# Two rows of h open every layer, and the 64 leftover tokens of batch 0 go behind the first 256 of batch 1

## The chip, the cores and the metric

The kernel runs on one core of a Trainium2 chip. The number that counts is the device time in microseconds (us) of one execution; lower is better. A core has engines that run side by side, each through its own list of instructions: PE (matrix products; PEld is its weight load), DVE (vector), ACT (scalar functions), POOL and SP. SP issues most of the DMA transfers. Results of PE land in PSUM, in banks of 128x512 fp32 values, from where ACT or DVE must carry them away before a bank is used again.

## What is computed

Attention over 4 batches, 8 heads, 576 tokens and 64 values a head, where each token keeps its 32 largest scores, and then two layers of a feed-forward network over all 2304 tokens:

```
scores = scale * np.matmul(q, k.transpose(0, 1, 3, 2))
kth = np.partition(scores, -top_k, axis=-1)[..., -top_k:-top_k + 1]
scores = np.where(scores >= kth, scores, -1000000000.0)
attn = softmax of scores;  x = attn @ v, as (2304, 512)
h = np.maximum(x @ w_in, 0.0);          x = h * h @ w_out          # layer 0
h = x @ w_in;  g = np.maximum(0.01 * h, h);  out = g @ w_out       # layer 1
```

Both layers have 512 features in and out and 2048 between them.

## The kernel before

**Attention.** Two heads make a head pair, so there are four head pairs (hp 0 to 3), and the output of head pair c is the 128-feature chunk c of x. `UNITS` lists (batch, first token, tokens); each unit is worked head pair by head pair, in tiles of 128 rows of scores by 576 keys, 144 tiles in all. Two tiles make a pair, 72 pairs in all, and the program is written in slots, 16 to a pair. In each pair DVE finds the 32 largest of every row with 8 MAX8 and 6 MATCH_REPLACE8 (lines 846 and 848). ACT then makes the exponentials (lines 303 and 307), PE transposes them (lines 321 and 334), ACT and DVE carry the transposes to PT or PTs (lines 326 to 344), and PE multiplies by v (line 405 or 416). Batches 2 and 3 have their scores computed during the first 245 slots, kept in DRAM (`sd`) and loaded again later; the others have theirs computed about two pairs ahead (line 285). Units numbered below `NATIVE` multiply by v in plain fp32 (`av`, line 405), the others in two fp32r parts, a high and a low one (`av_split`, line 416), for which v is split into two parts first (`load_v`, `split_v`).

**Feed-forward layers.** Tokens are cut into six `BLOCKS` of 512, 256, 384, 512, 256 and 384. A phase (j, layer) of block j has 16 steps f. Step f makes one row of h: 12 matmuls of a chunk of x (high part xh, low part xl) with the weights wi (line 592). ACT and POOL make gh and gl from it (lines 602 to 618), and one step later 12 (or fewer) matmuls add these into the accumulators acc (lines 635 and 637). At the end of layer 0 ACT and DVE write the accumulators back into x as xh and xl (lines 648 and 649), and layer 1 reads that. The phases run in the order (0,0), (0,1), (1,0), (1,1), (2,0), (2,1), (3,0), (3,1), (4,0), (5,0), (4,1), (5,1). The row h has one PSUM bank, the accumulators have four. In the phases (0,0) and (0,1) every step also converts its weights from 64-bit values (ACT lines 512, 521 and 532, DVE lines 527 and 528, called bits here, POOL line 533) and stores them in DRAM (`wd`); later phases load them from there.

**What sets the order.** A block's phases are written into the program once the block is full; the loop deals out three matmuls at a time at a rate that is meant to end when the next block is full, and writes what is left when it is. Attention work has a higher priority (`SOON`). From that program a list scheduler makes one fixed order for each engine, and each engine then goes through its order. In the order before, block 1 takes the 64 last tokens of batch 0 and 192 of batch 1, and 64 tokens are left over for block 2 (`spill`, `unspill`).

Of the kernel before, what the change touches and what calls it, by code (L numbers as in the profile page):

```python
# [8 lines left out]
F = mybir.dt.float32  # L9
# [3 lines left out]
OP = mybir.AluOpType  # L13
# [11 lines left out]


UNITS = [
    (0, 0, 256), (0, 256, 256), (0, 512, 64), (1, 0, 256), (1, 256, 320),
    (2, 0, 256), (3, 0, 256), (2, 256, 320), (3, 256, 320),
]  # L30

BLOCKS = [512, 256, 384, 512, 256, 384]

SETS = (0, 1, 0, 1, 0, 2)

# [2 lines left out]
SPILL = 128  # L38


NATIVE = 3

EARLY = (2, 3)
FILL = (2, 245)
# [13 lines left out]
LEAD = 24  # L58

SOON = 100  # L60
CONVP = 30

HI_SET = (0, 1, 2, 3, 4, 5, 6, 7, 8, 9, 10, 11, 12, 13, 14, 15)
# [17 lines left out]
def topk_attention_moe_moe2_kernel(  # L81
# [52 lines left out]
    for u in units:  # L134
        for hp in range(NHP):
            n = u["n"]
            uh = dict(u=u, hp=hp, n=n, b=u["b"], first=(u["t0"] == 0), ti=len(tiles), idx=len(uhs),
                      c0=P * (hp % 2) if n == 64 else 0)
# [12 lines left out]
    NPAIRS = len(tiles) // 2  # L151

    def direct(uh):
        return uh["b"] not in EARLY

    for i, uh in enumerate([uh for uh in uhs if direct(uh)]):
        uh["di"] = i

    def split(uh):
# [37 lines left out]
    def at(slot, fn, *a):  # L197
        events.setdefault(slot, []).append((fn, a))
# [68 lines left out]
    def scores(t, half):  # L267
        uh = t["uh"]
        d = uh["qs"]
        kt = KT[uh["b"], uh["hp"]]  # L270
        if half == 0:
            if direct(uh):
                t["s"] = sbufs[t["i"] % NS]
            else:
                t["s"] = ahead.tile([P, S], F, tag="stage", name="stage", bufs=NST)
        ks = slice(half * HALF, (half + 1) * HALF)
        mm = [(x[:, h, c:c + P], kt[:, h, ks]) for h, c in t["parts"] for x in d]
        if not direct(uh):
            ps = stage_psum.tile([P, 512], F, tag="sp", name="sp", bufs=SPB)
        elif uh["b"] == 0:  # L280
            ps = stage_psum.tile([P, 512], F, tag="sd", name="sd", bufs=SDB)
        else:
            ps = bank()
        for i, (l, r) in enumerate(mm):
            PE.matmul(ps[:, 0:HALF], lhsT=l, rhs=r, start=i == 0, stop=i == len(mm) - 1)
        ACT.activation(t["s"][:, ks], ps[:, 0:HALF], AF.Copy, scale=0.125)  # L286
        if half == 1 and not direct(uh):
            t["sd"] = dram.tile([P, S], F, tag=f"sd{t['i']}", name=f"sd{t['i']}")
            SP.dma_start(t["sd"], t["s"])

# [279 lines left out]
    def moe(j, layer):  # L570
# [6 lines left out]
        for f in range(NF + LAG):  # L577
            conv = iter(())
            if f < NF:
# [2 lines left out]
                conv = w_convert(si + 2)  # L582
                w_load(si + 2)
                wi, wo = wt.pop(si)
                h = late["psum"].tile([P, 512], F, tag="h", name="h", bufs=1)
                cnt = 0
# [4 lines left out]
                for w, c, y in mm:  # L591
                    PE.matmul(h[:, 0:n], lhsT=wi[:, w, c * P:(c + 1) * P], rhs=x[c][y][:, 0:n], start=cnt == 0,  # L592
                              stop=cnt == 3 * NK - 1)
                    cnt += 1
                    if cnt % MQ == 0 and cnt < 3 * NK:
                        next(conv, None)
                        yield
                gh = late["mlp"].tile([P, 512], R, tag="gh", name="gh", bufs=2)
                gl = late["mlp"].tile([P, 512], R, tag="gl", name="gl", bufs=2)
                a = late["mlp"].tile([P, 512], F, tag="ga", name="ga", bufs=2)  # L600
# [60 lines left out]
    used = {}  # L661
    opened = 16 * (max(uh["last"] for uh in uhs if not split(uh)) // 2) + 35

    def score_slot(ti):
        return 16 * (ti // 2) - DLEAD + 5 * (ti % 2)

    def after(z, *keys):
        return max([z] + [used[k] + 1 for k in keys if k in used])

    order = []  # L670
    for uh in uhs:
        b, hp, i = uh["b"], uh["hp"], uh.get("di")
        z = score_slot(uh["ti"])
        if uh["first"] and direct(uh):
            st = {"i": i}
            st["n"] = len(order)
            order.append(b)
            z0 = after(z - 62, ("kraw", st["n"] - KRB), *[("KT", x, hp) for x in range(b)])
            at(z0, load_k, b, hp, st)
            for h in range(2):  # L680
                at(z0 + 12 * h + 11, split_k, b, hp, st, h)
            used["kraw", st["n"]] = z0 + 23
            assert z0 + 24 <= z
        if (b, hp) not in vdone or split(uh) and VTB < NHP:
            assert not uh["u"]["i"] < NATIVE <= units[max(x["i"] for x in units if x["b"] == b)]["i"]
            vdone.add((b, hp))
            zv = z + DLEAD + 4
# [16 lines left out]
        used["q", i] = used["KT", b, hp] = score_slot(uh["last"]) + 2  # L704

    later_uhs = {}
    for uh in uhs:
# [44 lines left out]
    for p in range(NPAIRS):  # L752
# [1 line left out]
        pairs.append(pr)  # L754
        z = 16 * p
        for i, t in enumerate(pr["t"]):
            if direct(t["uh"]):
                at(z - DLEAD + 5 * i, scores, t, 0)
                at(z - DLEAD + 2 + 5 * i, scores, t, 1)
            else:  # L760
                at(z - LEAD + i, load_s, t)
            if i == 0:
                at(z + 14, shifts, pr)
            at(z + 14 + i, drop, pr, i)
# [157 lines left out]
```

## Time and profile before

| | us |
|---|---|
| median of 3 runs | 1200.16 |
| lowest and highest run | 1199.25, 1202.18 |
| the profiled execution | 1201.19 |
| its span, first to last instruction | 1199.4 |
| end of the last MAX8 of the 72 pairs | 958.3 |
| first matmul of phase (3,0), block 3 | 731.77 |

PE is busy 1130.8 us of the span, DVE 945.1, ACT 796.4, POOL 678.9; the granted clock of TensorE averages 0.983. Up to about 965 us attention and the feed-forward phases run together; what follows is feed-forward work alone. A row of the timeline gives the start, the length, engine, line, the operation, what it writes and reads, the shapes, how many were merged, and in brackets how long the engine was idle just before and what ended that.

### The profile page before, as it was taken

Reading aid. Unit: us, or ns where it says so; the run is one execution under the profiler, and the core shown is the slowest. Engines: PE = TensorE matmul, PEld = TensorE weight load, DVE = VectorE, ACT = ScalarE, POOL = GpSimd, SP = SyncE. Lnnn points to the kernel's source line nnn. Section 1 sums busy time; section 2 is a strip of 40 time slices with the busy share of each in tenths; the row PEclk is TensorE's granted clock in tenths of the full one; section 3 lists DMA queues with packets and bytes.
Section 4 is the critical chain, followed back from the end, with each engine's and each line's share of the span. In section 5 each row is a group of like instructions: output and inputs, shape, how many; then the busy total and the mean of one; then the engine's idle time right before and its main releaser. Section 6 shows DMA issues by size and latency. Waiting matters only on the chain.

```text
span 1199.4 us, 20071 instructions
## 1 busy us (share of the span) xinstructions
PE 1130.8 (94%) x6388; PEld 989.3 (82%) x6388; DVE 945.1 (79%) x1944; ACT 796.4 (66%) x1787; POOL 678.9 (57%) x922
## 2 busy tenths in 40 slices
PE   5899958999899999999998999999999999999997
PEld 4777846887677789988998997888788899998896
DVE  7999999879879899999999999999999910110121
ACT  6999979789889977766656676555666653334322
POOL 7967575778788875467665664555455543005200
PEclk9999988999999999999998999999999999999999
DMA  9868565679889888899987888676677589779973
GB/s 309 277 213 266 201 218 214 234 290 338 305 296 326 281 298 288 282 333 369 326 308 251 283 279 265 206 232 221 203 231 232 184 277 369 249 250 345 353 253 124
DMA packets 105914, 323.24 MB, mean 270 GB/s; under 512 B 16977, under 2 KB 25169, under 8 KB 101713
## 3 DMA queue, kind: packets, MB, share of 16 engines
q1 hardware_dynamic: 103168, 317.24, 77.6%
q10 hardware_dynamic: 2640, 4.72, 1.1%
q8 instruction: 52, 0.85, 0.3%
q14 instruction: 54, 0.43, 0.1%
HBM read 254.54 MB, written 67.37 MB: 268 GB/s over the span
## 4 chain that ended last, share of the span: by engine, by line
PE 69%; ACT 10%; DVE 10%; DMA 5%; POOL 3%; issue 2%; ACTq 0%; SPq 0%; POOLq 0%; DVEq 0%
PE h L592 28%; PE acc L637 14%; PE acc L635 14%; DVE m L846 4%; PE att L416 4%; PE att L321 3%; DVE w L848 3%; PE att L405 2%; DMA wraw<-in_w_dram 2%; ACT e L303 1%; DMA kraw<-in_k_dram 1%; ACT e L307 1%; DMA out_dram<-y 1%; ACT s L286 1%; ACT stage L286 1%
## 5 line engine op out<-in xcount | busy, mean ns | idle before, releaser
L592 PE MATMUL h<-xh,wi 128*128 128x512 f32 (+2 forms) x1280 | 351.8, 347 | 8.6 <-ACT ga L602 3.5
L846 DVE MAX8 m<-w 128x8 f32<-128x576 f32 x432 | 313.6, 747 | 1.3
L592 PEld LDWEIGHTS h<-xh,wi 128*128 128x128 f32 x1280 | 227.3, 191 | 37.1 <-ACT ga L602 5.0
L848 DVE MATCH_REPLACE8 w<-m,w 128x576 f32<-128x576 f32 x288 | 213.5, 743 | 0.8
L592 PE MATMUL h<-xl,wi 128*128 128x512 f32 (+2 forms) x640 | 207.1, 342 | 2.7 <-DVE xl L649 2.6
L618 POOL TENSOR_TENSOR gl<-ga,gh 128x512 fp32r<-128x512 f32 (+2 forms) x160 | 163.0, 1019 | 43.3 <-ACT gh L617 38.9
L635 PE MATMUL acc<-gh,wo 128*128 128x512 f32 (+2 forms) x768 | 157.4, 342 | 0.3 <-ACT y L652 0.3
L637 PE MATMUL acc<-wo,gh 128*128 128x512 f32 x576 | 151.9, 398 | 2.5 <-ACT gh L617 2.5
L615 POOL TENSOR_TENSOR ga<-ga,gb 128x512 f32<-128x512 f32 (+2 forms) x80 | 81.5, 1018 | 122.3 <-ACT gb L614 122.3
L635 PEld LDWEIGHTS acc<-gh,wo 128*128 128x128 f32 x768 | 127.1, 189 | 12.4 <-ACT y L652 0.8
L592 PEld LDWEIGHTS h<-xl,wi 128*128 128x128 f32 x640 | 121.4, 191 | 14.9 <-DVE xl L649 4.3
L303 ACT ACTIVATE e<-s,m 128x576 f32<-128x576 f32 x144 | 112.4, 781 | 31.1 <-DVE m L846 24.2
L637 PEld LDWEIGHTS acc<-wo,gh 128*128 128x128 f32 x576 | 103.9, 188 | 22.9 <-ACT gh L617 4.0
L307 ACT ACTIVATE e<-e,nb 128x576 f32<-128x576 f32 x144 | 110.9, 774 | 5.7 <-POOL nb L297 5.5
L604 POOL TENSOR_TENSOR ga<-ga 128x512 f32<-128x512 f32 (+2 forms) x80 | 66.3, 828 | 82.3 <-ACT gh L603 79.6
L846 DVE MAX8 m<-s 128x8 f32<-128x576 f32 x144 | 103.7, 747 | 7.9 <-ACT s L286 5.9
L848 DVE MATCH_REPLACE8 w<-m,s 128x576 f32<-128x576 f32 x144 | 107.0, 743 | 0.6
L321 PE MATMUL att<-ident,e 128*128 128x128 f32 x576 | 88.1, 279 | 18.1 <-ACT e L307 12.8
L321 PEld LDWEIGHTS att<-ident,e 128*128 128x128 f32 x576 | 69.7, 143 | 31.2 <-ACT e L307 17.4
L602 ACT ACTIVATE ga<-h 128x512 f32<-128x512 f32 (+2 forms) x80 | 39.1, 488 | 80.2 <-PE h L592 77.8
L316 POOL TENSOR_SCALAR e<-e,rc 128x576 f32<-128x576 f32 x108 | 79.7, 751 | 16.6 <-DVE rc L312 15.4
L617 ACT ACTIVATE gh<-ga 128x384 fp32r<-128x384 f32 (+2 forms) x112 | 58.6, 523 | 42.2 <-POOL ga L615 32.2
(94 smaller groups left out, 2133.4 us busy)
## 6 DMA issues: line engine op xcount, KB each, us to landing
wi<-wd SPq DMA_DIRECT2D x160, 512.0 KB, 5.2
wo<-wd SPq DMA_DIRECT2D x160, 512.0 KB, 5.4
wraw<-in_w_dram SPq DMA_DIRECT2D x32, 1024.0 KB, 6.6
sd<-stage SPq DMA_DIRECT2D x72, 288.0 KB, 3.3
s<-sd SPq DMA_DIRECT2D x72, 288.0 KB, 4.6
wd<-wi SPq DMA_DIRECT2D x32, 512.0 KB, 5.6
wd<-wo SPq DMA_DIRECT2D x32, 512.0 KB, 6.0
kraw<-in_k_dram SPq DMA_DIRECT2D x16, 576.0 KB, 4.5
```

Source lines behind the costliest of these rows:

```text
L303: ACT.activation(t["e"], t["s"], AF.Prelu, bias=pr["m8"][:, i, 31:32], scale=-1.0, alpha=1.0 / FAR)
L307: ACT.activation(e, e, AF.Exp, bias=pr["nb"][:, i:i + 1], scale=-FAR, accum_out=pr["sum"][:, i:i + 1])
L316: POOL.tensor_scalar(e, e, pr["rc"][:, i:i + 1], 1.0, op0=OP.mult, op1=OP.mult)
L321: PE.transpose(ps[:, j * P:(j + 1) * P], t["e"][:, j * P:(j + 1) * P], ident)
L592: PE.matmul(h[:, 0:n], lhsT=wi[:, w, c * P:(c + 1) * P], rhs=x[c][y][:, 0:n], start=cnt == 0, stop=cnt == 3 * NK - 1)
L604: POOL.tensor_tensor(a[:, 0:n], a[:, 0:n], a[:, 0:n], op=OP.mult)
L615: POOL.tensor_tensor(a[:, 0:n], a[:, 0:n], b[:, 0:n], op=OP.subtract)
L618: (DVE if j >= GLD else POOL).tensor_tensor(gl[:, 0:n], a[:, 0:n], gh.bitcast(F)[:, 0:n], op=OP.subtract)
L635: PE.matmul(acc[c][:, 0:n], lhsT=wo[:, w, cs], rhs=g[:, 0:n], start=first, stop=last)
L637: PE.matmul(acc[c], lhsT=g[:, cs], rhs=wo[:, w, :], start=first, stop=last)
L846: cur["dve"] = DVE.max(out=m8[:, x, 8 * r:8 * r + 8], in_=t["s"] if r == 0 else t["w"])
L848: cur["dve"] = DVE.match_replace(out=t["w"], in_to_replace=m8[:, x, 8 * r:8 * r + 8], in_values=t["s"] if r == 0 else t["w"], imm_value=NEG)
```

## The change

- `UNITS`: the unit of the 64 last tokens of batch 0 moves behind the first 256 tokens of batch 1. Block 1 is then exactly these 256 tokens, block 2 is 64 + 320 tokens, and nothing is spilled at block 1.
- `NATIVE` goes from 3 to 2: units 0 and 1 stay plain, and the 64-token unit is now split in two parts as the units after it. Its v is loaded, split and stored a second time.
- `KEPT`: the scores of these 64 tokens are computed while the keys of batch 0 are still there, stored in DRAM and loaded again, as for batches 2 and 3.
- `OPENING`: at step 0 of a phase two rows of h (steps 0 and 1) are computed together, chunk by chunk, the second one in a bank of the accumulators; step 1 then has no matmuls of h left.
- `SEAM`: the evictions from acc to xh and xl at the end of layer 0 get a higher priority.

```diff
 UNITS = [
-    (0, 0, 256), (0, 256, 256), (0, 512, 64), (1, 0, 256), (1, 256, 320),
+    (0, 0, 256), (0, 256, 256), (1, 0, 256), (0, 512, 64), (1, 256, 320),
...
+OPENING = (
+    ((0, 0),), ((1, 0),), ((0, 1),), ((2, 0),), ((1, 1),), ((3, 0),), ((2, 1), (3, 1)),
+)
...
-NATIVE = 3
+NATIVE = 2
+KEPT = 3
...
+SEAM = 400
...
-            if direct(uh):
+            if direct(uh) and not kept(uh):
                 t["s"] = sbufs[t["i"] % NS]
...
-        if half == 1 and not direct(uh):
+        if half == 1 and (kept(uh) or not direct(uh)):
             t["sd"] = dram.tile([P, S], F, tag=f"sd{t['i']}", name=f"sd{t['i']}")
...
                 if f == 0:
-                    mm = [(w, c, 0) for w in range(2) for c in range(NK)] + [(0, c, 1) for c in range(NK)]
+                    two = [late["psum"].tile([P, 512], F, tag="acc" if r else "h", name="h", bufs=4 if r else 1)
+                           for r in range(2)]
+                    ws = [wi, wt[si + 1][0]]
+                    mm = [(r, w, c, y) for part in OPENING for r in range(2) for c, y in part
+                          for w in ((0,) if y else (0, 1))]
+                elif f > 1:
+                    two = [late["psum"].tile([P, 512], F, tag="h", name="h", bufs=1)]
+                    ws = [wi]
+                    mm = [(0, 0, c, y) for c in range(NK) for y in range(2)] + [(0, 1, c, 0) for c in range(NK)]
                 else:
-                    mm = [(0, c, y) for c in range(NK) for y in range(2)] + [(1, c, 0) for c in range(NK)]
+                    mm = []
...
-                ACT.activation(xh[:, 0:n], acc[c][:, 0:n], AF.Copy)
-                DVE.tensor_tensor(xl[:, 0:n], acc[c][:, 0:n], xh.bitcast(F)[:, 0:n], op=OP.subtract)
+                with tc.high_priority(offset=SEAM):
+                    ACT.activation(xh[:, 0:n], acc[c][:, 0:n], AF.Copy)
+                    DVE.tensor_tensor(xl[:, 0:n], acc[c][:, 0:n], xh.bitcast(F)[:, 0:n], op=OP.subtract)
...
+            if kept(t["uh"]):
+                at(t["uh"]["zs"], scores, t, 0)
+                at(t["uh"]["zs"] + 2, scores, t, 1)
+            if kept(t["uh"]) or not direct(t["uh"]):
+                at(z - LEAD + i, load_s, t)
```

The first place is PE where block 0 becomes full. `e` are exponentials, `rc` their sums' reciprocals, `PT,VN` is the product with v for the last head pair, and `h<-xh0` with 128x512 are rows of h in phase (0,0). Before, with the last product and what follows it:

```order
L405 MATMUL att_2499<-PT_115,VN_1069 128x256 x9
L285 MATMUL att_2533<-KT_2187,q00_77 128x288
L285 MATMUL att_2533<-KT_2187,q10_78 128x288
L355 MATMUL att_2484<-ident_66,rc_2295 128x128 x2
L405 MATMUL att_2499<-PT_115,VN_1069 128x256
L285 MATMUL att_2563<-KT_2187,q00_77 128x288
L285 MATMUL att_2563<-KT_2187,q10_78 128x288
L321 MATMUL att_2585<-ident_66,e0_107 128x128 x4
L592 MATMUL h_2543<-xh0_649,wi_2350 128x512 x5
L592 MATMUL h_2543<-xl0_650,wi_2350 128x512 x4
```

Three of the 12 matmuls of the first row stand ahead of the last product, nine behind it. Now the same place of the changed kernel:

```order
L424 MATMUL att_2561<-PT_115,VN_1069 128x256 x8
L374 MATMUL att_2546<-ident_66,rc_2371 128x128 x2
L424 MATMUL att_2561<-PT_115,VN_1069 128x256 x2
L304 MATMUL att_2597<-KT_1962,q01_83 128x288
L304 MATMUL att_2597<-KT_1962,q11_84 128x288
L304 MATMUL att_2642<-KT_1962,q01_83 128x288
L304 MATMUL att_2642<-KT_1962,q11_84 128x288
L618 MATMUL h_2612<-xh0_649,wi_2420 128x512 x2
L618 MATMUL h_2613<-xh0_649,wi_2500 128x512 x2
L618 MATMUL h_2612<-xl0_650,wi_2420 128x512
L618 MATMUL h_2613<-xl0_650,wi_2500 128x512
L618 MATMUL h_2612<-xl0_650,wi_2420 128x512
```

Eight matmuls on the last chunk of x are left for two rows; the 16 on the first three chunks stand ahead of these lines.

The second place is DVE where phase (1,0) ends and its accumulators are written back (`xl1<-acc`). `m8` and `w` belong to the search for the 32 largest, and `s4` and `s5` are the score tiles of a pair that is just being begun. Before:

```order
L848 MATCH_REPLACE w_6428<-m8_6424,s3_104 128x576
L846 MAX m8_6424<-w_6427 128x8
L846 MAX m8_6424<-w_6428 128x8
L312 RECIPROCAL rc_6222<-sum_6221 128x2
L846 MAX m8_6592<-s4_105 128x8
L848 MATCH_REPLACE w_6427<-m8_6424,w_6427 128x576
L649 TENSOR_TENSOR xl1_2826<-acc_5236,xh1_2825 128x256
L649 TENSOR_TENSOR xl1_2826<-acc_5237,xh1_2825 128x256
```

Counted from the start of DVE's order, 278 of its 576 MAX8 stand ahead of the first of these `xl1` lines. After:

```order
L872 MAX m8_6192<-s4_105 128x8
L872 MAX m8_6050<-w_6054 128x8
L346 TENSOR_TENSOR PTs_2609<-att_5938,PTs_2609 128x4x128
L874 MATCH_REPLACE w_6195<-m8_6192,s4_105 128x576
L346 TENSOR_TENSOR PTs_2609<-att_5956,PTs_2609 128x4x128
L874 MATCH_REPLACE w_6054<-m8_6050,w_6054 128x576
L676 TENSOR_TENSOR xl1_3215<-acc_5075,xh1_3214 128x256
L676 TENSOR_TENSOR xl1_3215<-acc_5076,xh1_3214 128x256
```

Here 256 MAX8 stand ahead of the write-back: it has moved up by 22 MAX8, not quite three pairs, in DVE's order.

The third place is PE where block 3 becomes full and phase (3,0) opens; `acc` with `wo` is the end of phase (2,1), `PTs,VT` the product with v, `h<-xh1` with 128x512 the new phase. Before:

```order
L637 MATMUL acc_8265<-wo_9032,gl_9193 128x512
L637 MATMUL acc_8266<-wo_9032,gl_9193 128x512
L637 MATMUL acc_8267<-wo_9032,gl_9193 128x512
L416 MATMUL att_9230<-PTs_3112,VT_8843 128x256
L321 MATMUL att_9290<-ident_66,e0_107 128x128 x4
L321 MATMUL att_9324<-ident_66,e1_108 128x128 x4
L334 MATMUL att_9352<-ident_66,e0_107 64x128
L334 MATMUL att_9352<-ident_66,e1_108 64x128
L592 MATMUL h_9266<-xh1_7292,wi_9102 128x512 x5
```

The last product with v for block 3 stands beside the last matmuls of phase (2,1). After, a few lines behind the end of (2,1), which now comes one whole head pair earlier:

```order
L435 MATMUL att_9158<-PTs_2609,VT_8919 128x256 x9
L340 MATMUL att_9214<-ident_66,e2_109 128x128 x4
L340 MATMUL att_9239<-ident_66,e3_110 128x128 x4
L353 MATMUL att_9265<-ident_66,e2_109 64x128
L353 MATMUL att_9265<-ident_66,e3_110 64x128
L435 MATMUL att_9311<-PTs_2609,VT_8919 128x256 x9
L618 MATMUL h_9353<-xh1_7376,wi_9194 128x512
```

Both products of the last head pair now stand behind the end of (2,1), with only attention work and the first 16 matmuls of the new phase around them.

## Rows read from the trace of the kernel before

**Rows 1.** The page, part 1: busy us (share of the span) xinstructions.

```profile
PE 1130.8 (94%) x6388; PEld 989.3 (82%) x6388; DVE 945.1 (79%) x1944; ACT 796.4 (66%) x1787; POOL 678.9 (57%) x922
```

**Rows 2.** Windows of two stretches: length, busy us by engine, PE clock, DMA share, GB/s.

```profile
core 0: us, PE busy (x) PEld busy (x) DVE busy (x) ACT busy (x) POOL busy (x), PEclk, DMA share, GB/s
...
316.00:419.00 103.00, 97.71 (x457) 78.22 (x457) 90.43 (x171) 95.23 (x183) 86.00 (x85) 0.98 0.88 307
...
502.00:739.00 237.00, 230.18 (x1387) 213.16 (x1385) 234.27 (x495) 151.22 (x344) 146.41 (x214) 0.99 0.87 303
```

**Rows 3.** What DVE waited for, 193 to 419 us: total us, times, longest.

```profile
DVE wc L527 <- ACT att L521: 19.0, 15, 4.2
DVE m L846 <- ACT s L286: 3.6, 5, 1.4
```

**Rows 4.** The same for DVE, 419 to 739 us, all there is.

```profile
DVE m L846 <- ACT s L286: 1.0, 1, 1.0
DVE PTs L327 <- ACT PTs L326: 0.2, 1, 0.2
DVE xf L422 <- ACT tmp L421: 0.2, 1, 0.2
```

**Rows 5.** Timeline of DVE: first write-back of (1,0), block 3 full, write-back of (3,0).

```profile
501.89 0.75 DVE L649 TENSOR_TENSOR xl<-acc,xh 128x256 fp32r<-128x256 f32 x2
...
738.57 0.43 DVE L422 TENSOR_TENSOR xf<-att,tmp 64x256 f32<-64x256 f32 x1
...
849.74 0.68 DVE L649 TENSOR_TENSOR xl<-acc,xh 128x512 fp32r<-128x512 f32 x1
```

**Rows 6.** What PE waited for, 193 to 502 us: first and last of thirteen.

```profile
PE att L334 <- ACT s L286: 3.0, 1, 3.0
...
PE att L285 <- ACT s L286: 0.2, 1, 0.2
```

**Rows 7.** Timeline of PE where phase (0,0) opens.

```profile
194.34 1.43 PE L592 MATMUL h<-xh,wi 128*128 128x512 f32 x5 [0.49 <-ACT xh L437]
195.61 1.07 PE L592 MATMUL h<-xl,wi 128*128 128x512 f32 x4
197.70 0.66 PE L321 MATMUL att<-ident,e 128*128 128x128 f32 x4 [1.02 <-DVE wc L528]
198.84 0.50 PE L592 MATMUL h<-xh,wi 128*128 128x512 f32 x1 [0.49 <-ACT ga L602]
```

**Rows 8.** Timeline of PE between (0,0) and (0,1), and where (1,0) ends.

```profile
316.24 2.87 PE L592 MATMUL h<-xh,wi 128*128 128x512 f32 x8 [0.18 <-ACT xh L648]
...
319.95 1.09 PE L592 MATMUL h<-xl,wi 128*128 128x512 f32 x2 [0.39 <-DVE xl L649]
...
322.69 0.79 PE L592 MATMUL h<-xh,wi 128*128 128x512 f32 x1 [1.28 <-ACT gb L614]
...
498.71 0.64 PE L635 MATMUL acc<-gl,wo 128*128 128x256 f32 x4
```

**Rows 9.** The chain that ended last, pieces: start us, us, what.

```profile
215.78 4.83 PE att L405 x40
...
322.69 4.56 PE h L592 x12
...
330.48 2.75 PE h L592 x12
```

**Rows 10.** Timeline of PE: prices of a score matmul, a transpose and a split product.

```profile
434.82 0.69 PE L285 MATMUL att<-KT,q 128*128 128x288 f32 x4
...
521.19 1.03 PE L321 MATMUL att<-ident,e 128*128 128x128 f32 x8
...
538.42 1.34 PE L416 MATMUL att<-PTs,VT 128*128 128x320 f32 x8
```

**Rows 11.** Timeline of PE where block 3 becomes full and where (2,0) has ended.

```profile
650.40 1.15 PE L592 MATMUL h<-xl,wi 128*128 128x384 f32 x2 [1.95 <-DVE xl L649]
...
739.06 0.64 PE L334 MATMUL att<-ident,e 128*64 128x128 f32 x2 [1.52 <-DVE xf L422]
```

More of the change, by code (lines that the diff above doesn't have):

```diff
@@ L136, in topk_attention_moe_moe2_kernel @@
             n = u["n"]
-            uh = dict(u=u, hp=hp, n=n, b=u["b"], first=(u["t0"] == 0), ti=len(tiles), idx=len(uhs),
+            uh = dict(u=u, hp=hp, n=n, b=u["b"], first=(u["t0"] == 0), i0=u["i"], ti=len(tiles), idx=len(uhs),
                       c0=P * (hp % 2) if n == 64 else 0)
@@ L154, in direct, with kept, score_slot @@
         return uh["b"] not in EARLY
-    for i, uh in enumerate([uh for uh in uhs if direct(uh)]):
+    def kept(uh):
+        return uh["u"]["i"] == KEPT
+    def score_slot(ti):
+        return 16 * (ti // 2) - DLEAD + 5 * (ti % 2)
+    for uh in uhs:
+        uh["zs"] = score_slot(uh["ti"])
+        if kept(uh):
+            ahead_of = [x for x in uhs if x["b"] == uh["b"] and x["hp"] == uh["hp"] and x["i0"] < uh["i0"]][-1]
+            uh["zs"] = score_slot(ahead_of["last"]) + 5
+    in_time = sorted([uh for uh in uhs if direct(uh)], key=lambda uh: uh["zs"])
+    for i, uh in enumerate(in_time):
         uh["di"] = i
@@ L584, in moe @@
                 wi, wo = wt.pop(si)
-                h = late["psum"].tile([P, 512], F, tag="h", name="h", bufs=1)
-                cnt = 0
                 if f == 0:
-                    mm = [(w, c, 0) for w in range(2) for c in range(NK)] + [(0, c, 1) for c in range(NK)]
-                else:
-                    mm = [(0, c, y) for c in range(NK) for y in range(2)] + [(1, c, 0) for c in range(NK)]
[L591 to L595, printed above, removed]
+                    two = [late["psum"].tile([P, 512], F, tag="acc" if r else "h", name="h", bufs=4 if r else 1)
[7 more added lines that the diff above has]
+                    mm = [(0, 0, c, y) for c in range(NK) for y in range(2)] + [(0, 1, c, 0) for c in range(NK)]
+                else:
+                    mm = []
+                for cnt, (r, w, c, y) in enumerate(mm):
+                    mine = [i for i, m in enumerate(mm) if m[0] == r]
+                    PE.matmul(two[r][:, 0:n], lhsT=ws[r][:, w, c * P:(c + 1) * P], rhs=x[c][y][:, 0:n],
+                              start=cnt == mine[0], stop=cnt == mine[-1])
+                    if cnt % MQ == MQ - 1 and cnt < len(mm) - 1:
                         next(conv, None)
                         yield
+                h = two.pop(0)
                 gh = late["mlp"].tile([P, 512], R, tag="gh", name="gh", bufs=2)
@@ L662, in topk_attention_moe_moe2_kernel @@
     opened = 16 * (max(uh["last"] for uh in uhs if not split(uh)) // 2) + 35
-    def score_slot(ti):
-        return 16 * (ti // 2) - DLEAD + 5 * (ti % 2)
     def after(z, *keys):
@@ L670, in topk_attention_moe_moe2_kernel @@
     order = []
-    for uh in uhs:
+    for uh in in_time + [uh for uh in uhs if not direct(uh)]:
         b, hp, i = uh["b"], uh["hp"], uh.get("di")
-        z = score_slot(uh["ti"])
+        z = uh["zs"]
         if uh["first"] and direct(uh):
@@ L684, in topk_attention_moe_moe2_kernel @@
         if (b, hp) not in vdone or split(uh) and VTB < NHP:
-            assert not uh["u"]["i"] < NATIVE <= units[max(x["i"] for x in units if x["b"] == b)]["i"]
             vdone.add((b, hp))
-            zv = z + DLEAD + 4
+            zv = score_slot(uh["ti"]) + DLEAD + 4
             if split(uh):
@@ L703, in topk_attention_moe_moe2_kernel @@
         used["qraw", i] = z1 + 4
-        used["q", i] = used["KT", b, hp] = score_slot(uh["last"]) + 2
+        used["q", i] = used["KT", b, hp] = (z if kept(uh) else score_slot(uh["last"])) + 2
     later_uhs = {}
@@ L756, in topk_attention_moe_moe2_kernel @@
         for i, t in enumerate(pr["t"]):
-            if direct(t["uh"]):
+            if kept(t["uh"]):
[3 more added lines that the diff above has]
+                at(z - LEAD + i, load_s, t)
+            else:
                 at(z - DLEAD + 5 * i, scores, t, 0)
                 at(z - DLEAD + 2 + 5 * i, scores, t, 1)
-            else:
-                at(z - LEAD + i, load_s, t)
             if i == 0:
```

## Prediction

> **What bounds the kernel now.** I read the page's shares first: PE is busy 94% of the span, DVE 79% [rows 1]. An average hides stages, so I went to the windows and, for each, to the list of what DVE and PE waited for. Three stages come out.
>
> Up to 193 us DVE works through the pairs that fill block 0, and PE has nothing to do but attention. From 193 to 419 us the phases (0,0) and (0,1) run beside attention and convert their weights. DVE waits there for ACT, 19.0 us in 15 waits for the bits and 3.6 for scores [rows 3]; ACT is busy 95.2 of the 103 us from 316, POOL 86.0, PE 97.7 [rows 2]. PE sets the pace here, ACT close behind, and DVE has time over. From 419 to 739 us it is the other way round: DVE waits three times, 1.4 us in all [rows 4], and is busy 234.3 of the last 237 us [rows 2]. PE waits there too (1.95 us at the seam from (2,0) to (2,1) [rows 11]), but these waits end nothing: block 3 is full when DVE has done its work, at 738.57 us [rows 5], and PE, idle for 1.52 us, waits for exactly that [rows 11]. The write-back of (3,0) at 849.74 us [rows 5] comes again from a DVE that was busy throughout. Behind it PE alone counts.
>
> So the end is: the time at which DVE stops waiting, plus DVE's work from there to the write-back of (3,0), plus some 345 us of PE. A PE wait between 419 and 739 us costs nothing now, and nothing is won by taking it away.
>
> **The change, part by part.** By the orders, the last instruction that DVE must wait for PE with moves to the end of phase (1,0), to its write-back. I add up when PE gets there, and what DVE still has to do.
>
> Start: DVE's order has two instructions fewer ahead of block 0's last piece, so 0.8 us less; the first row of h on the last chunk goes from 194.3 [rows 7] to 193.5 us.
>
> PE from there to the end of (1,0) takes 304.8 us before: 194.3 to 499.1 [rows 7, 8]. Counted in the two orders over this stretch:
> - 13 fewer matmuls of h, done while the last chunk is awaited, at 0.23 (12 in 2.75 us [rows 9]): -3.0.
> - 42 fewer score matmuls, as 22 fewer MAX8's worth of pairs fall in here, at 0.14 (4 take 0.69, so 0.17 at most [rows 10]): -5.9.
> - 22 fewer transposes at 0.11 (8 in 1.03, so 0.13 at most [rows 10]): -2.4.
> - The 64 tokens' plain products, 80 pieces at 0.12 (40 in 4.83 us [rows 9]), go: -9.7.
> - In their place 72 split products of 64 columns, which no row shows. A product of 320 columns takes 0.17 at most (8 in 1.34) and a transpose of 128 columns 0.13 [rows 10]; below the transpose nothing in the trace goes. That gives 7.9 to 12 us; I take 0.11, the price of the narrower: +7.9.
> - 18 fewer split products of 320 columns at 0.15: -2.7. Those of 256 columns and the h of 256 columns come out even.
>
> Sum -15.8. Stalls taken away: at the opening of (0,0) PE waits 1.02 and 0.49 us before gh is ready [rows 7]; in the new order 12 matmuls of step 2 and 8 transposes stand there: -1.5. At the seam from (0,0) to (0,1) it waits 0.18, 0.39 and 1.28 us [rows 8], and the next 12 matmuls take 4.56 us instead of 2.75 [rows 9] as the granted clock has dropped to its lower level (1.2 GHz; the mean from 316 us is 0.98 [rows 2]) after the idle time: -3.6. The second row of h needs no bank of the first and covers its eviction. The other waits of the thirteen [rows 6], the longest of 3.0 us, come from an ACT and a POOL that are nearly full, and stay.
>
> What is added there hides: the second load, split and store of batch 0's v (about 1 MB for each of four head pairs) is DMA and POOL work, as is the storing and loading of four score tiles; DMA stands at 0.88 [rows 2] and can take it while PE has slack. If that cover is gone, (1,0) waits for weights: 4 MB at the 307 GB/s of [rows 2] are 13 us at worst, 0 at best; I take 0, since the loads fall behind the conversion's peak.
>
> So (1,0) ends at 193.5 + 304.8 - 15.8 - 5.1 = 477.4, and its write-back starts 0.5 us later, at 477.9 instead of 501.9: 24.0 us earlier.
>
> DVE from there to a full block 3: before 236.7 us [rows 5], in which its order holds 155 MAX8 and 116 MATCH_REPLACE. After, the write-back stands 22 MAX8 earlier, and 175 MAX8 and 129 MATCH_REPLACE are left to do. By the first that is 13% more (30.5 us), by the second 11% (26.5); I take 28. So 24.0 earlier and 28 longer: block 3 is full 4 us later, at 742.6. From there to the write-back of (3,0) it is 111.2 us before [rows 5] and about 1 more (74 MAX8 for 73, 57 MATCH_REPLACE for 55). PE gets to the end of (2,1) about 20 us ahead of DVE and waits; its seams are better, and that is hidden. Behind the write-back PE's order is 0.7 us shorter: 4.0 + 1.0 - 0.7 = +4.3.
>
> Against its own time, the profiled execution of 1201.19 us (span 1199.4 and 1.8 around it), the sum gives 1205.5. That execution is 1.0 above the median of 1200.16, so I forecast a median of **1204.5 us**.
>
> **A rule read against this.** DVE, not PE, sets the end between 419 and 849 us: three waits, 1.4 us [rows 4]. The Trainium skill (Perfetto Trace Analysis, section Identifying the Most-Contended Engine) says to optimize first the engine with the highest occupancy, for TensorE judged by its weight loads. By [rows 1] that is PE by either measure, and the change closes PE's gaps, so by this rule they would come off the end, as in the first rival below; for the stage from 419 us the trace speaks against it.
>
> **The rivals.**
> 1. PE bounds throughout, and DVE's later order does not matter. Then all seam stalls come off: 5.1 us so far, 1.95 us at (2,0) [rows 11] and 1.52 at block 3 with what follows them at the lower clock, some 15 in all, and 2 us of PE work: 1183. For it: 94% [rows 1]. Against it: [rows 4].
> 2. The stalls of PE in 193 to 499 us mostly vanish, as ACT has fewer pairs to serve beside the conversions. The thirteen waits [rows 6] are some 13 us together; with the lower clock behind them 17. Without them (1,0) ends at 465, DVE is 12 us further, and the time is 1192. This is on the other side; it decides from 9 us of stalls taken away, where DVE breaks even. Against it: the waits are mostly for ACT, and ACT and POOL have nearly the same work in less time.
> 3. Even: 8 to 14 us of stalls go, 1196 to 1202, say 1200. The change then does what it says, and DVE gives it all back.
> 4. The conversions get in each other's way: the same work of ACT, POOL and DMA in some 20 us less. PE stalls grow by 8 to 10 us: 1214.
>
> **How the numbers follow.** Forecast (2 to 8 us of stalls gone, 1202 to 1209): 0.42, a quarter of it within 0.3% of before. Rival 1 0.04, rival 2 0.18, rival 3 0.23, rival 4 0.13. About 0.3% (3.6 us) is what a measurement of this kernel can tell from no change: faster 0.22, same 0.33, slower 0.45. The range reaches from rival 2 to rival 4, 1191 to 1214; outside are rival 1 and half of rival 4 and a little of rival 2, under 0.2.
>
> **What the profile after would show.** Right: phase (0,1) over by about 412 us, the write-back of (1,0) near 478 with an idle DVE just before it, no waits of DVE worth the name from there to block 3, that full at 740 to 746, and PE idle some 15 us or more ahead of it; the write-back of (3,0) near 855. Wrong: DVE reaching the write-back of (1,0) after PE (then DVE's pairs before it cost more than I think), block 3 full before 735 (rival 2), or DVE waiting for PE behind 500 us. If the seam at (0,0) still waits over 1 us, the opening does not cover it.

## The result, and the profile after

The changed kernel takes 1216.83 us (median of 4 runs, 1216.07 to 1219.11), the kernel before beside it 1201.07. The ratio is 1.0136, 95% interval 1.0116 to 1.0156: slower, where I forecast +0.4% and a range that ends at 1214. The direction was right, the size was not. The profiled execution took 1216.8 us, its span is 1215.0, against the 1201.19 and 1199.4 that the sum was made against.

The page's shares, part 1, hardly differ from [rows 1] (busy us, share, instructions):

```profile
PE 1134.1 (93%) x6376; PEld 992.2 (82%) x6376; DVE 947.7 (78%) x1956; ACT 799.2 (66%) x1791; POOL 685.8 (56%) x926
```

No engine but POOL has more to do worth the name (7 us), so most of the 15.6 us is idle time. On DVE they are easy to find. The windows of DVE alone, first of the kernel before, then of the changed one (length, DVE busy, clock of PE, DMA share, GB/s): from 192 to 455 us, and from the start to the first matmul of phase (3,0) on the last chunk of x, that is, to a full block 3.

```profile
192.00:455.00 263.00, 232.63 (x449) 0.99 0.83 291
...
0.00:739.50 739.50, 695.03 (x1427) 0.98 0.82 282
```

```profile
192.00:455.00 263.00, 218.85 (x423) 0.98 0.92 325
...
0.00:755.00 755.00, 695.29 (x1434) 0.97 0.84 287
```

Read the second line of each: up to a full block 3 DVE does 695 us of work in either kernel. The difference of 15.5 us between 739.5 and 755.0 is idle time but for 0.3 (44.5 before, 59.7 after), and the first lines hold 13.8 of it: 30.4 us idle before, 44.2 after. From a full block 3 to the end of the span both need 460 us. This is the account that I use for every run below: **a full block 3 = DVE's 695 us + DVE's idle time, and some 460 us behind it.** In the runs that leave all of DVE's work in, this work ranges from 691 to 703 us, with the number of MAX8 of the next pairs that its order lets in ahead, and the rest from 455 to 468.

What DVE waited for in these 263 us (us in all, times, longest), which answers to [rows 3] and the start of [rows 4]:

```profile
DVE wc L546 <- ACT att L540: 14.2, 10, 4.5
DVE m L872 <- ACT s L305: 11.5, 6, 3.7
DVE rc L331 <- POOL sum L330: 6.4, 3, 5.0
DVE xf L441 <- POOL xl L459: 3.4, 2, 2.1
```

The bits come out better than before, but scores, sums and the products of the 64 tokens (`xf`) now end waits. Behind 455 us there is again next to nothing, as in [rows 4]. The loss stands between 374 and 455 us. There PE has no room left and DVE has (the columns of [rows 2]; before, then after):

```profile
374.00:455.00 81.00, 78.76 (x459) 68.02 (x458) 76.35 (x150) 69.68 (x147) 63.78 (x79) 1.00 0.86 296
```

```profile
374.00:455.00 81.00, 79.31 (x513) 72.72 (x512) 52.68 (x109) 56.49 (x130) 53.25 (x69) 0.96 0.86 307
```

The end of (1,0) on PE, the three places of [rows 5] on DVE, and PE's first matmul of (3,0) on the last chunk (timelines; in brackets the idle time before and what ended it):

```profile
484.68 0.64 PE L661 MATMUL acc<-gl,wo 128*128 128x256 f32 x4
```

```profile
487.90 1.41 DVE L676 TENSOR_TENSOR xl<-acc,xh 128x256 fp32r<-128x256 f32 x4
...
754.12 0.43 DVE L441 TENSOR_TENSOR xf<-att,tmp 64x256 f32<-64x256 f32 x1
...
864.35 0.68 DVE L676 TENSOR_TENSOR xl<-acc,xh 128x512 fp32r<-128x512 f32 x1
```

```profile
755.04 0.79 PE L618 MATMUL h<-xh,wi 128*128 128x512 f32 x1 [4.96 <-ACT xh L456]
```

The write-back of (1,0) comes 14.0 us earlier than before and not 24; PE had ended the phase at 485.3, and DVE, without any idle time just ahead, came 2.6 us after it. Its last wait of note was for scores at 449.44 us.

### The profile page after: what moved, and what is told of

Its sections match the earlier page's. It is cut to its first block, busy times and chain, and to the rows that moved or that the text cites. A ratio compares the mean times of both kernels' runs of the same rounds, so it can differ in the third digit from the quotient of the medians.

```text
span 1215.0 us, 20085 instructions
## 1 busy us (share of the span) xinstructions
PE 1134.1 (93%) x6376; PEld 992.2 (82%) x6376; DVE 947.7 (78%) x1956; ACT 799.2 (66%) x1791; POOL 685.8 (56%) x926
## 4 chain that ended last, share of the span: by engine, by line
PE 55%; DVE 5%; ACT 3%; DMA 2%; issue 1%; POOL 0%; ACTq 0%; POOLq 0%
PE h L618 23%; PE acc L661 12%; PE acc L663 11%; PE att L435 4%; PE att L340 3%; DVE m L872 2%; DVE w L874 2%; DMA out_dram<-y 1%; PE att L304 1%; PE att L353 1%; DMA wi<-wd 1%; ACT PTs L345 1%; DVE PTs L346 0%; ACT y L679 0%; ACT e L322 0%
## 5 line engine op out<-in xcount | busy, mean ns | idle before, releaser
L618 PE MATMUL h<-xh,wi 128*128 128x512 f32 (+2 forms) x1280 | 347.5, 345 | 17.0 <-ACT xh L456 9.9
L663 PEld LDWEIGHTS acc<-wo,gh 128*128 128x128 f32 x576 | 103.8, 188 | 25.1 <-ACT gh L643 5.7
L872 DVE MAX8 m<-s 128x8 f32<-128x576 f32 x144 | 104.4, 753 | 15.7 <-ACT s L305 12.7
L335 POOL TENSOR_SCALAR e<-e,rc 128x576 f32<-128x576 f32 x112 | 82.5, 749 | 21.1 <-DVE rc L331 20.1
L435 PE MATMUL att<-PTs,VT 128*128 128x256 f32 (+2 forms) x504 | 85.8, 301 | 4.5 <-DVE PTs L346 1.3
L661 PE MATMUL acc<-gl,wo 128*128 128x512 f32 (+2 forms) x384 | 87.7, 346 | 1.9 <-POOL gl L644 1.9
```

The lines of the kernel that those rows point to most:

```text
L335: POOL.tensor_scalar(e, e, pr["rc"][:, i:i + 1], 1.0, op0=OP.mult, op1=OP.mult)
L435: PE.matmul(ps, lhsT=l, rhs=r, start=i == 0, stop=i == len(mm) - 1)
L618: PE.matmul(two[r][:, 0:n], lhsT=ws[r][:, w, c * P:(c + 1) * P], rhs=x[c][y][:, 0:n], start=cnt == mine[0], stop=cnt == mine[-1])
L661: PE.matmul(acc[c][:, 0:n], lhsT=wo[:, w, cs], rhs=g[:, 0:n], start=first, stop=last)
L663: PE.matmul(acc[c], lhsT=g[:, cs], rhs=wo[:, w, :], start=first, stop=last)
L872: cur["dve"] = DVE.max(out=m8[:, x, 8 * r:8 * r + 8], in_=t["s"] if r == 0 else t["w"])
```

## Experiments

Two theories stood against each other. **Pace**: block 1 now counts as full at slot 402 instead of 434, so the program deals (0,0) and (0,1), 256 portions of three matmuls, out over 127 slots instead of 159, 2.02 a slot instead of 1.61; PE's order then has these phases ahead of attention work that DVE needs, DVE waits, and gives nothing back later because it is the bound from 455 us on. **The unit of 64 tokens**: four head pairs in two pairs of DVE's, each with its v, its single buffers and its chain of PE, ACT, DVE and POOL. A third suspect was the opening. SEAM is none: written without it, the program has the same order on all five engines, instruction by instruction.

All ratios are against the kernel before on the same chip, with 95% intervals. The columns behind them are from the profiled execution: DVE's idle time between 192 and 455 us, the time at which block 3 is full, and the rest of the span from there. d1, v1 and p0 leave out work that the result needs and are there for the time alone.

| run | ratio | idle 192 to 455 | block 3 full | rest |
|---|---|---|---|---|
| before | 1 | 30.4 | 739.5 | 459.9 |
| changed kernel | 1.0136 (1.0116 to 1.0156) | 44.2 | 755.0 | 460.0 |
| u1_units | 1.0249 (1.0223 to 1.0274) | 48.5 | 762.9 | 468.0 |
| u2_opening | 1.0031 (1.0014 to 1.0048) | 40.8 | 751.5 | 456.7 |
| r3_before_pace | 1.0130 (1.0099 to 1.0160) | 43.0 | 748.5 | 467.1 |
| r1_defer417 | 1.0140 (1.0114 to 1.0165) | 46.8 | 755.3 | 460.4 |
| x1_defer417_xf2 | 1.0092 (1.0074 to 1.0110) | 43.5 | 752.4 | 460.4 |
| x3_after_xf2 | 1.0091 (1.0068 to 1.0115) | 43.9 | 754.2 | 458.1 |
| v1_no_v64 | 1.0108 (1.0075 to 1.0142) | 42.5 | 748.0 | 461.3 |
| p0_less_pe_early | 1.0082 (1.0062 to 1.0101) | 39.3 | 745.2 | 461.9 |
| p1_more_pe_late | 1.0096 (1.0068 to 1.0125) | 44.5 | 753.5 | 459.4 |
| d1_less_dve_late | 1.0000 (0.9984 to 1.0016) | 44.3 | 743.5 | 457.4 |
| r0_swap (402) | 1.0095 (1.0074 to 1.0116) | 42.4 | 755.7 | 455.7 |
| r8_swap425 | 1.0039 (1.0024 to 1.0054) | 30.1 | 743.8 | 460.7 |
| r4_swap441 | 0.9979 (0.9963 to 0.9995) | 28.3 | 746.0 | 454.7 |
| r2_swap449 | 1.0003 (0.9989 to 1.0017) | 24.9 | 743.4 | 457.1 |
| r5_swap449_noopen | 1.0000 (0.9979 to 1.0021) | 24.9 | 741.2 | 459.3 |
| r7_swap441_noopen | 1.0050 (1.0034 to 1.0067) | 25.1 | 744.3 | 461.5 |
| r6_before_defer449 | 1.0045 (1.0030 to 1.0061) | 33.1 | 743.2 | 460.5 |
| r9_swap441_xf2 | 1.0016 (1.0001 to 1.0031) | 27.1 | 745.1 | 456.8 |

Two limits of this table. A profiled execution can lie 4 us off its kernel's median (u2_opening 1210.35 for 1206.24, p0_less_pe_early 1208.88 for 1213.05). And the rows were not measured side by side: the kernel before took 1201.07 us beside the changed kernel and 1202.76 to 1203.67 beside the runs, and p1_more_pe_late, which has the changed kernel's order up to some 570 us and more work behind, came out 0.4% below it. So 0.4% below the changed kernel is by itself no gain.

**Which part of the change loses.** u1_units takes the opening and SEAM out of the changed kernel:

```diff
-                if f == 0:
-                    two = [late["psum"].tile(... tag="acc" if r else "h" ...) for r in range(2)]
...
+                if f == 0:
+                    mm = [(w, c, 0) for w in range(2) for c in range(NK)] + [(0, c, 1) for c in range(NK)]
```

> The changed kernel with the opening of two rows and the eviction priority undone; the new order of units, the split 64 tokens and the kept scores stay. Theory (pace): block 1 is now full after pair 25 and not after pair 27, so the phases (0,0) and (0,1) have to be over in 8 pairs of DVE's instead of 10; DVE waits there and has the missing pairs to do later, when it sets the end. The units alone do that: 1213 to 1219 us, DVE idle for some 25 us between 374 and 455 us. Rival (seams): the new opening puts PE, ACT and POOL out of step; without it the time is that of before, about 1201.

u2_opening puts the same hunk, with its table `OPENING`, into the kernel before.

> The kernel before with only the opening of two rows added. Pace: PE's seams behind 419 us are hidden under DVE, those ahead of it give 1 to 4 us: 1197 to 1201. Seams: the opening carries the loss: 1210 to 1217.

The units alone lose 2.5%, more than I expected of them, and the opening takes 1.1% of that back; alone on the kernel before it loses 0.3%, between its two forecasts. So the opening is not the culprit, and its worth depends on what it stands beside. With the units it takes 7.9 us off the time at which block 3 is full, and 8.0 off the rest: without it 511 MAX8 stand ahead of the write-back of (3,0) in DVE's order, with it 505.

**The pace alone.** r3_before_pace is the kernel before with one line more:

```diff
+    rate[0] = sum(quanta(*ph) for ph in groups[0]) / 127
```

> The kernel before with one number changed: (0,0) and (0,1) are dealt out over 127 slots, as in the changed kernel, instead of 159; units, opening and everything else as before. Pace: PE's order then has the end of (0,1) ahead of the attention of pairs 25 to 27, DVE waits 8 to 14 us more between 192 and 455 us, 1208 to 1215. Rival (unit of 64 tokens): without that unit in its new place nothing happens, 1199 to 1204.

1.0130, as much as the whole change, with units, opening and the rest as they were. Its window, and what heads the list of DVE's waits in it, which stood at 19.0 us in [rows 3] and got no longer up to 455 us:

```profile
192.00:455.00 263.00, 220.03 (x422) 0.97 0.83 286
```

```profile
DVE wc L527 <- ACT att L521: 27.6, 14, 4.0
```

DVE does 12.6 us less in the window than before, almost what the changed kernel lost (13.8). Block 3 is full 9.0 us later, and 7.2 us come behind it, as DVE's order now has 511 MAX8 ahead of the write-back of (3,0) and not 506. That the pace alone can lose as much as the change is shown by this run, and without the change's transfers: the DMA share in the window is 0.83 as before, where the changed kernel has 0.92. Its course is another one, though: its (1,0) is written back at 507.48 us, 5.6 later than before, and in the changed kernel 14.0 earlier.

**The changed kernel with a slower pace.** r1_defer417 lets block 1 count as full only at slot 417, one slot ahead of the first x of block 2, whose x goes where block 0's was, so that (0,1) must be over by then:

```diff
-            ready.append(blk)
+            if blk["idx"] != 1:
+                ready.append(blk)
...
+    at(DEFER, lambda: ready.append(blocks[1]))
+    rslot[1] = DEFER
```

> The changed kernel, in which block 1 counts as full 15 slots later, just ahead of the first x of block 2, so that (0,0) and (0,1) are dealt out over 143 slots instead of 127 (159 before). Pace: half of the loss comes back, 1207 to 1212, and DVE waits some 10 us less between 374 and 455 us. Rival (the unit of 64 tokens): its second split of v, its kept scores and its single buffers make DVE wait whatever the pace is: 1215 to 1219.

A miss: no gain. The waits only moved. From 320 to 374 us DVE is idle 8.9 us where it was 4.1, from 374 to 420 us 10.7 where it was 15.5, and from 420 to 455 us, at the 64 tokens, 14.1 where it was 12.8. So I looked at that unit by itself.

**The unit of 64 tokens.** In v1_no_v64 it takes the split v that is still there:

```diff
+        if kept(uh):
+            VT[b, hp] = VT[1, NHP - 1]
+            return
...
-            if split(uh):
+            if split(uh) and not kept(uh):
```

> The changed kernel without the second loading, splitting and storing of batch 0's v: the 64 tokens are multiplied by the split v of batch 1's last head pair, which is still there, so their rows of the output are others. That takes 8 splits from ACT (0.45 us each), 8 from POOL (0.85) and 16 transfers away. Rival (unit of 64 tokens): four head pairs' v in two pairs is what holds ACT and the scores up; DVE's waits between 419 and 455 us, 12 us now, go to under 4, and the time to 1203 to 1209. Pace: DVE is ahead of PE there in any case and waits elsewhere instead, 1214 to 1218.

The waits that it was to remove are still there (DVE busy 21.8 of the 35 us from 420, where it was 22.2); what it gained, it gained ahead of 420 us and by 4 MAX8 fewer ahead of a full block 3 in its order (427 for 431), and its interval meets that of the changed kernel. So the second split of v is not by itself what DVE waits for. r0_swap moves the unit behind the 320 tokens of batch 1:

```diff
-    (0, 0, 256), (0, 256, 256), (1, 0, 256), (0, 512, 64), (1, 256, 320),
+    (0, 0, 256), (0, 256, 256), (1, 0, 256), (1, 256, 320), (0, 512, 64),
...
-KEPT = 3
+KEPT = 4
```

> The changed kernel with the 64 tokens behind the 320 of batch 1 instead of ahead of them; block 1 is full at the same slot. Pace: (0,0) and (0,1) still have 8 pairs, 1213 to 1219. Unit of 64 tokens: its work moves to some 500 us, where DVE is the one that is waited for and ACT and POOL have time over; the 12 us of waits behind 419 us go, 1203 to 1209.

It lands between the two forecasts, next to that of the pace. The same window, 420 to 455 us, in the changed kernel and in r0_swap:

```profile
420.00:455.00 35.00, 22.21 (x50) 0.90 0.92 328
```

```profile
420.00:455.00 35.00, 33.46 (x71) 1.00 0.87 296
```

The 12.8 us of idle time there go to 1.5, but ahead of 420 us DVE waits 9 us more, so that block 3 is full no earlier (755.7). What the time gains (0.4%) lies behind it (455.7 for 460.0). Moved out of the way, the unit's waits came back elsewhere, as long as the pace was the same. x1_defer417_xf2 and x3_after_xf2 give the sums of this unit, and of every split unit, two buffers, at slot 417 and in the changed kernel as it is:

```diff
-            uh["xf"] = late["pool"].tile([P, 320], F, tag="xf", name="xf", bufs=1)
-            uh["tmp"] = late["pool"].tile([P, 320], F, tag="tmp", name="tmp", bufs=1)
+            uh["xf"] = late["pool"].tile([P, 320], F, tag="xf", name="xf", bufs=2)
+            uh["tmp"] = late["pool"].tile([P, 320], F, tag="tmp", name="tmp", bufs=2)
```

> The changed kernel deferred to slot 417, with two buffers instead of one for tmp and for the sums xf. If it is the single buffers of the 64-token unit that take back what the slower pace gives: DVE's waits between 420 and 455 us go from 14 to under 9, 1208 to 1213. If the unit waits for PE, which has the end of (0,1) and then (1,0) in front: 1217 to 1222.

> The changed kernel with two buffers instead of one for tmp and xf, nothing else. If the single buffers make DVE wait by themselves: 4 to 6 us, as at slot 417, 1211 to 1213. If they only matter where the pace is slower: 1215 to 1218.

Both gain some 5 us by their times, each beside its forecasts and not much more than p1 with its added work. The waits of `xf` for POOL, 3.4 us in the changed kernel, are gone in x3. Block 3 is full 2.9 us earlier in x1 and 0.8 in x3, so that of the gain at most 3 us are the unit's own; the rest lies behind block 3 or between one execution and the median.

**Swap and pace together.** r2, r4 and r8 are r0_swap with block 1 full at slots 449, 441 and 425. That is possible there because 320 tokens take longer to reach block 2 than 64.

> The same, and block 1 counts as full only just ahead of the first x of block 2, at slot 449: (0,0) and (0,1) get 175 slots, more than before (159), (1,0) and (1,1) get 145. Pace: DVE's waits between 192 and 455 us fall below those of before (30 us), 1192 to 1201. Unit of 64 tokens alone: as the kernel that is only swapped.

> The kernel with 320 ahead of 64 tokens, block 1 counting as full at slot 441 instead of 449. By the two orders two MAX8 and two MATCH_REPLACE fewer stand ahead of a full block 3 (434 and 324 against 436 and 326), some 3 us of DVE. Pace, with DVE's waits as in the run at 449: 1197 to 1202. If the 8 slots count as much as the others did (10 us for 47): 1202 to 1206.

> The kernel with 320 ahead of 64 tokens, block 1 counting as full at slot 425: between 402 (1212.8) and 441 (1201.7). Pace, step by step: 1204 to 1210. If it is a step at some slot, either 1211 to 1214 or 1200 to 1203.

One number is changed in steps: 402, 425, 441, 449 give 1.0095, 1.0039, 0.9979, 1.0003, and DVE's idle time in the window 42.4, 30.1, 28.3, 24.9 us.

Beyond 441 it gains no more: at 449 DVE's order has 436 MAX8 ahead of a full block 3 and not 431 as in the changed kernel, and DVE's work to there is 703 us, not 695. In the other direction the kernel before wins nothing with 15 slots more:

> The kernel before with block 1 counting as full 15 slots later, at slot 449, just ahead of the next x: (0,0) and (0,1) get 175 slots instead of 159. Pace: some 5 us less waiting of DVE ahead of 455 us; as many MAX8 stand ahead of block 3 (432 for 433), so the time falls to 1194 to 1200. If the pace only costs when it is too fast: 1200 to 1204.

It lost 0.45%, so 159 slots are not too few there, and "the slower, the better" is refuted.

**The opening at a right pace.** r5 and r7 are r2 and r4 without it.

> The run at slot 449 without the opening of two rows. If the opening helps by covering stalls of PE that DVE has to wait for, it is worth less here than the 14 us between units alone and the whole change, as PE is less ahead of time's need: 1200 to 1207. If it is worth the same: 1213 to 1219.

> The kernel with 320 ahead of 64 tokens at slot 441, without the opening of two rows. Ahead of block 3 stand 3 MAX8 and 2 MATCH_REPLACE fewer than with it (431 and 322 against 434 and 324), some 4 us of DVE; with the same waits 1196 to 1201. If the opening is worth something at this pace: 1203 to 1208.

Nothing at 449, 0.7% at 441, where all of the difference lies behind a full block 3 (461.5 against 454.7 us). Between a full block 3 and the write-back of (3,0) DVE has 75 MAX8 and 106.2 us of work in r7, and 71 and 102.3 in r4; at 449 it is 74 in both runs. Why the scheduler deals them out so, I can't say. r9 adds the second buffers to r4:

> The kernel with 320 ahead of 64 tokens at slot 441 with two buffers for tmp and xf. There DVE hardly waits for either, and three MAX8 more stand ahead of the write-back of (3,0) in its order (508 for 505): 1200 to 1205. If the buffers help the rest too: 1196 to 1199.

It gains nothing (1.0016 against 0.9979), as the first of its two forecasts had it. The best version is therefore r4_swap441 at 0.9979, under the 0.3% that I had named as measurable.

**Which engine sets the end.** Late, from 455 us to a full block 3, by taking work from DVE and by giving work to PE:

```diff
+            elif 10 <= i < 12 and 38 <= p < 48:
+                pass
```

> The changed kernel without the third MATCH_REPLACE of both tiles in pairs 38 to 47 (the search there finds the third eight twice): 20 instructions of 0.42 us less for DVE, 8.4 us, at about 540 to 680 us. If DVE sets the end there: 1208 to 1209. If PE does: 1216 to 1217, no change.

```diff
+                if (j, layer) == (2, 0) and 3 <= f < 13:
+                    for _ in range(4):
+                        PE.matmul(two[0][:, 0:n], lhsT=ws[0][:, 0, 0:P], rhs=x[0][0][:, 0:n], start=True, stop=True)
```

> The changed kernel with 4 more matmuls of 384 columns ahead of the row of h in ten steps of phase (2,0); their result is overwritten. 40 of 0.17 us, 6.9 us more for PE between 520 and 640 us. If DVE alone sets the end there: 1215 to 1219. If PE does: 1222 to 1226.

d1 gained 1.4% by the ratios, 16 us, and 14.1 by the spans (1200.9 for 1215.0), not the 8.4 that I had given it: I had priced MATCH_REPLACE by its line's mean, in which the short value loads count too. The lines grouped, DVE in d1 from 455 to 743 us, give its real length (the mean in ns stands behind the busy time):

```profile
L876 DVE MATCH_REPLACE8 w<-m,w 128x576 f32<-128x576 f32 x79 | 58.6, 743 | 0.3
```

20 of 0.74 us are 15 us, and with each of them a value load of 0.08 us goes; DVE's busy time fell by 13.9 us. p1 put 40 matmuls more on PE and was not slower at all. In the stretch that the two runs touch, some 560 to 680 us, DVE is the bound, as the prediction said of 419 to 849 us.

Early, p0_less_pe_early takes work from PE in (0,1):

```diff
+                    if (j, layer) == (0, 1):
+                        mm = mm[:-NK]
```

> The changed kernel without the last four matmuls of h (the weights' low part) in each step from the third on of phase (0,1): 56 matmuls of 0.23 us, 13 us less for PE between 305 and 400 us. If PE holds DVE up there (pace): phase (1,0) ends 8 to 13 us earlier, DVE waits as much less, 1204 to 1209. If ACT, POOL or the v of the 64 tokens do: 1213 to 1217.

About half of the 13 us of PE came off: (1,0) is written back at 480.55 us, 7.3 earlier, and DVE is idle 39.3 us for 44.2 in the window. The ratio, 1.0082 against 1.0136, is little clear of the 0.4% of p1. So PE holds DVE up there in part. DVE still waits 16.1 us for ACT's bits; what sets these was not tested.

## Why the prediction was wrong

1. **The start and PE's matmuls: right.** Block 0's last x stands at 191.66 us, 1.0 earlier for the 0.8 that I gave. Counted by kind at the same prices, the matmuls between a full block 0 and the write-back of (1,0) come to 15.7 us less than before; I had 15.8. They come to 19.4 less up to the last h of (0,1) and to 3.8 more behind it, where the 64 tokens now stand.

2. **The stalls of PE: wrong by 3.5 us.** I took off 5.1 us. With them (0,1) would have ended at 434.0 - 0.8 - 19.4 - 5.1 = 408.7; it ended at 412.2. That is the 412 that I named as a sign, but only because I had not split the sum there. PE's idle time from the first row of h on the last chunk to the end of (0,1) is 13.1 us, before it was 11.7: the waits stayed, in other places. PE in the changed kernel where (0,0) opens, and between (0,0) and (0,1), against [rows 7] and [rows 8]:

```profile
203.94 0.53 PE L304 MATMUL att<-KT,q 128*128 128x288 f32 x2 [1.62 <-DVE PTs L346]
...
302.71 1.22 PE L618 MATMUL h<-xh,wi 128*128 128x512 f32 x4 [1.09 <-ACT xh L675]
305.14 0.47 PE L618 MATMUL h<-xh,wi 128*128 128x512 f32 x1 [1.22 <-DVE xl L676]
```

The opening covers the waits at (0,0) of [rows 7], and a score matmul that needs DVE waits 1.62 us instead. At the seam the two rows wait for the same evictions as one did, 1.09 and 1.22 us; only the lower clock behind it is gone (granted 1.00 from 302 to 312 us, before 0.53 from 322.6 to 326.2).

3. **PE from there to the end of (1,0): 4 us too short.** Before it took 65.3 us (434.0 to 499.35); with 3.8 more it should have been 69.1, and it was 73.1 (412.2 to 485.3). The 64 tokens stand here:

```profile
420.37 1.22 PE L661 MATMUL acc<-gh,wo 128*128 128x256 f32 x8 [1.61 <-ACT gh L629]
421.52 3.97 PE L435 MATMUL att<-PTs,VT 128*128 128x64 f32 x19
```

A microsecond behind an idle time of 1.61 us PE runs at its lower clock (1.2 GHz): the granted clock is 0.53 from 421.5 to 428.8 us and 1.00 from there to 455. 19 products of 64 columns take 3.97 us, where 10 take 1.20 at 442.81. But the 4 us came without the lower clock as well. The same place in p1_more_pe_late, which has the same order up to here and a granted clock of 1.00 from 420 to 455 us:

```profile
421.19 1.20 PE L664 MATMUL acc<-gh,wo 128*128 128x256 f32 x8 [1.61 <-ACT gh L632]
422.34 2.31 PE L435 MATMUL att<-PTs,VT 128*128 128x64 f32 x19
```

On PE its (1,0) ends at 485.36 us all the same (changed kernel: 485.32), and it is written back at 487.94 (487.90). What PE gains by the clock it loses at 431.88, where it waits 1.74 us for ACT's scores, and DVE waits for these scores 3.74 us (changed kernel: 3.70, at 431.25). ACT has the second load of the 64 tokens' v ahead of them in its order and waits for the transfer, 1.99 us in p1; in the changed kernel:

```profile
429.79 0.83 ACT L129 ACTIVATE VT<-vraw 128x320 fp32r<-128x320 f32 x2 [1.95 <-DMA vraw<-in_v_dram]
```

So "what is added there hides" was wrong too: I had counted this load as work of DMA and POOL alone. Its price is small, though: without it (v1) DVE still waits 4.60 us for the scores, which PE then finishes only at 427.84, and (1,0) is written back at 485.30 us, 2.6 earlier. At this place PE, ACT and the transfer end close together; p1 and v1 show that when one of them is quicker, the next one holds DVE. The range had this place at "0 to 13 us", for the weights of the phases, and I took 0.

4. **The failed step.** It is "the last instruction that DVE must wait for PE with moves to the end of phase (1,0)". Between 374 and 455 us DVE was idle 28.3 us, against 4.7 before, in front of bits, scores, sums and the 64 tokens' `xf`; it was last held up at 449.44 us, and had 38.5 us of work from there to the write-back, so that it came 2.6 us after PE's end of the phase. This is the sign that I had named (DVE at the write-back after PE), but not for the reason that I gave: DVE's pairs cost no more. Up to the write-back DVE did 27.4 us less work than before (432.8 for 460.2) and was idle 13.4 us more (55.1 for 41.7). My 24.0 us earlier left room for 3.4 us of idle time more. I had priced the waits of DVE in this stage by PE's end of phase alone and its added chain at 0. So the write-back came 10.0 us later than forecast, and every later time is shifted by it. PE's own end of the phase would have made it 7.9 us late (3.5, 4.0 and 0.4 in my reading of the time before).

5. **What follows is as forecast.** From the write-back of (1,0) to a full block 3: 266.2 us, forecast 236.7 + 28 = 264.7. PE had 4.96 us of idle time just ahead of it, where I had named 15. From there to the write-back of (3,0): 110.2, forecast 112.2. Behind it 350.6 us, forecast 349. With the 10.0 us that is 11.1 of the 11.3 us between the spans, 1215.0 and 1203.7 forecast. The move of some 22 MAX8 behind (1,0), the heart of the sum, was right to 1.5 us.

6. **The rivals.** Rival 4 came closest by its number (1214), and that is luck: its 8 to 10 us of stalls of PE more did not come (1.4 more up to the end of (0,1)), DVE's waits did. Rivals 1 to 3 fell: the stalls that they take off stayed. The rule of the Trainium skill (Perfetto Trace Analysis, section Identifying the Most-Contended Engine), to optimize the engine with the highest occupancy first, names PE by the shares of the whole span (93%, DVE 78%), and there the runs speak against it: less work for DVE shortened the time (d1), more for PE did not lengthen it (p1). By the occupancy of the stage from 455 to 640 us alone it names DVE (182.6 of 185 us; PE 179.1, its weight loads 171.4), and that agrees.

What is shown and what is not: that the pace of (0,0) and (0,1) can make a loss of this size is shown by r3, and with the unit moved, in four steps, by r0, r8, r4 and r2. That it makes the loss of the changed kernel itself is not shown: r1 gave it 15 slots more and gained nothing, and why stays open. Of the 64 tokens in their place, the second buffers bring 1 to 3 us ahead of block 3 (x1, x3), little more than the 1.5 us by which p1 and the changed kernel differ there; that the place itself costs more isn't shown, since without it (r0) the waits come back elsewhere. The lower clock at 421.5 us didn't reach the write-back: p1 has it at the same time without. The shares don't add up: r3 has neither the new units nor the opening, and part of what it loses lies behind block 3.

## What to carry over

When a buffer becomes full earlier, look at what must be over by then: here two phases lost a fifth of their slots, and an in-order engine then has their work in front of what the bound engine waits for. Make the account on the engine that sets the end, busy time and idle time up to the last place where others wait for it; work that stays the same leaves only the idle time to forecast, and each wait in that stage needs its own price, also of those that the change moves. A gain on an engine that is not the bound (the opening: from -1.1% to +0.3%) has no worth of its own and must be measured beside the rest.

## What the runs showed that I had not expected

- The same order with the same wait of PE (1.61 us) was followed by 7 us at the lower of the two clock levels in the changed kernel (granted 0.53, 0.21 us for a product of 64 columns) and by none in p1 (1.00, 0.12 us), and both wrote (1,0) back within 0.04 us of each other.
- A product of 64 columns takes 0.12 us at the higher clock (19 in 2.31 us in p1), about as long as one of 256 columns (8 in 1.10 us at 480.51).
- Left out of DVE's order, a MATCH_REPLACE8 of 128x576 is worth its full 0.74 us: 20 of them, with their value loads, took 14.1 us off the span.
- Program text that asks for a higher priority can leave every engine's order as it is (SEAM).
